# Retention scores and a Mish feed-forward on one core: block 2 of 11 takes the form that block 3 has

## The chip, the cores and the metric

The kernel runs on one core of one Trainium2 chip, as one launch. Its time is device microseconds of that core. Five engines take part, each with an instruction stream of its own that it works through in order: PE (TensorE, matmuls and weight loads), DVE (VectorE), ACT (ScalarE), POOL (GpSimd) and SP (SyncE, which here only issues DMAs). They wait for each other through semaphores: an instruction that waits holds up all that stands behind it on its engine.

## What is computed

`q`, `k` and `v` are (4, 8, 768, 64): 4 batches, 8 heads, 768 positions, 64 numbers each. A decaying state is updated at each position and read by `q`; the heads side by side give `x` of 3072 rows by 512. Then a feed-forward with Mish follows, with weights of 512x2048 and 2048x512.

```python
state = np.zeros((B, H, D, D), dtype=np.float32)
for t in range(S):
    state = gamma[None, :, None, None] * state + np.einsum('bhd,bhe->bhde', k[:, :, t], v[:, :, t])
    y[:, :, t] = scale * np.einsum('bhd,bhde->bhe', q[:, :, t], state)
x = attn_out.transpose(0, 2, 1, 3).reshape(B * S, H * D)
h = x @ w_in
sp = np.where(h > 20.0, h, np.log1p(np.exp(np.minimum(h, 20.0))))
return (h * np.tanh(sp)) @ w_out
```

## The kernel before

**Tiling.** The 768 positions of a batch are 6 chunks of 128, so there are 24 chunks, numbered 0 to 23 through all batches. They are worked in 11 blocks: block 0 has chunks 0 to 3, block n from 1 on has chunks 2n+2 and 2n+3. Block 2 thus has chunks 6 and 7, block 3 has 8 and 9, block 4 has 10 and 11, block 5 has 12 and 13. Chunk 11 is the last of batch 1 (`last_of_batch`), chunk 9 is not.

**The small matmuls.** For a block, 64x64 matmuls make the outer products of `k` and `v` (`outers`, L515, into the tile `u`, and of these DVE makes the states), the scores (`scores`, L507, into `at`) and then `y` in three parts: `past_of` from the states, `present_of(own)` and, after a wait for a DVE copy (`seen`, L660), the other half of `present_of` (all at L621). The scores are masked by DVE (`mask_two`, L604 or L609) before `present_of` reads them. The states after a block's second chunk come from `leave`, that is `state_of` (L570 to L581): an addition (L579) that reads `u`, and a product (L580). For the last chunk of a batch `state_of` returns before both.

**The feed-forward.** Both products are done with sums that save an eighth of the matmuls. The first (`full_in`, L973) takes 112 matmuls of 128x128 in groups, the second (`seven`, L1098, or `full_out`, L1215) 56 of 128x256. DVE makes the sums that the second needs: `sums_a` (L925, L926), `sums_b` (L930) and `sums_c` (L934).

**Where a block's small matmuls stand.** This is set by two numbers, `ONE, BACK = 3, 4`, and there are three forms:

- Blocks before `ONE` (1 and 2): the outer products and the scores of the next block stand inside this block's first product, by `get_ready` (L583), which ends with `settle` (the states, on DVE). `y` of the next block stands in `seven`, and is cut in two by half of a product of 256 columns.
- Block `ONE` (3): the same `get_ready` of block 4, and in `seven` the whole of `y` of block 4 with the outer products and scores of block 5 (`retain(4, 5)`, which calls `ready(5)`) in one piece.
- Blocks from `BACK` (4) on: no `get_ready`; in `full_out` the same piece, `retain(blk + 1, blk + 2)`.

**Banks of PSUM.** Up to block `BACK` the tiles `at` and `u` of a block share the pool `atps`. For blocks after `BACK`, `hold` (L530) closes that pool and opens two new ones in its place (`new_banks`), so their first tiles lie on the banks of the last `at` and `u` of `atps`: the writer waits until those have been read.

**Conversions and loads.** SP loads `q`, `k`, `v` of a chunk, POOL converts them (`casts_qk`: L440 for `q` and L454 for `k`; `casts_v`: L459), ACT takes some of the `k` (`cast_k`, L452), and a transposing DMA from SP (`turn_by_dma`, L464) turns `q` and `k` for the scores. The outer products read the converted `k` and `v` directly. POOL is held back in places by a copy of one column to `summed`: it waits for the DVE instruction that writes that column, and the conversions stand behind it. In `cast_load` (called at the head of block 2) chunk 10 is converted and the loads of 12 and 13 issued; `cast_behind(2, 3)` and the lines at L1152 and L1169 take chunks 11, 12 and 13.

**Matmuls cut in halves.** `IN_HALVES` and `HALVED` name products whose matmuls are issued as two of half the columns, each with a weight load.

Of the kernel before, what the change touches and what calls it, by code (L numbers as in the profile page):

```python
# [16 lines left out]
def kernel(  # L17
# [9 lines left out]
    nc = tc.nc  # L27
    B, H, S, D = q.shape
    d_model, d_ff = moe_w_in.shape
    P = 128  # L30
# [4 lines left out]
    TB = 512  # L35
# [84 lines left out]
    loaded, cast, qkts, ats, ams, states, mids, us, ys = {}, {}, {}, {}, {}, {}, {}, {}, {}  # L120
    xts, gts, wins, wouts, wtmps = {}, {}, {}, {}, {}
    gtiles, tmats, gsums = {}, [], []
    ONE, BACK = 3, 4
    EVEN, ODD = slice(0, NBP, 2), slice(1, NBP, 2)
    ROWS = [[slice(i, i + 1) for i in (0, 2, 1, 3)], [EVEN, ODD], [EVEN, ODD], [slice(0, NBP)]]
    whole, late_k = {}, []
    HALVED, DEFER = {6: (8, 8, 0, 0, 0)}, 6
    IN_HALVES = {0: range(NFB - 7, NFB), 1: range(NFB - 8, NFB)}
    FULL, SUMS_AT = (2, 3), {1: (4, 5, 5, 6)}
    in_makes = {}  # L130
    nload, ncast = [0], [0]
# [829 lines left out]
    def full_in(blk, last):  # L961
# [62 lines left out]
        for fn, p in ((first_of, 0), (first_of, 1), (fifth_of, 0), (fifth_of, 1)) if both else (  # L1024
                (first_of, 0), (fifth_of, 0), (first_of, 1), (fifth_of, 1)):
            fn(p)
        if late_k:
            g = first[blk] + 5
            store(1)
            cast_k(*late_k.pop(0))  # L1030
            turn_by_dma(g)
            casts_v(g - 1)
            casts_v(g)
            load_to(g + 3)
            store(1)
        settled = last or both
        if both:
            leave(blk)
# [32 lines left out]
        for p in two:  # L1071
            mm(pa[p], a(p, 1, 1), t[3])
            mish(p, 1, 0, pa[p])
        sums_a(blk, 1)

    def seven(blk, masks, hooks):
        n, hf = NFB // 2, d_model // 2
        px = pxps.tile([P, hf], FP32, name="o_ps", tag="px")
        pb = mmps.tile([P, hf], FP32, name="o_ps", tag="mm")
        osb = [  # L1080
            op.tile([P, d_model], FP32, name="osb", tag="osb", bufs=9) for _ in range(2)]

        def a(i, j):
            return lambda f: gts[blk, j * n + f][:, i * P:(i + 1) * P]

        def b(i, j):
            return lambda f: wouts[(i * n + f) // FPS][:, f % FPS, j * hf:(j + 1) * hf]

        def s(i):
            return lambda f: gsums[blk % 2][:, i - 1, f]  # L1090

        def t(i):
            return lambda f: tmats[(i - 1) // 2][:, (i - 1) % 2, f]

        def mm(o_ps, x, w, first=False, turn=0, part=slice(None), cols=slice(None)):
            for z in range(n)[part]:
                f = (z + turn) % n
                nc.tensor.matmul(  # L1098
                    o_ps[:, cols], x(f), w(f)[:, cols], start=first and z == 0, stop=z == n - 1,
                    skip_group_check=True)  # L1100

        def snap(o_ps, cols=slice(0, hf)):
            x = op.tile([P, hf], FP32, name="snap", tag="snap", bufs=3)[:, cols]
            nc.scalar.copy(x, o_ps[:, cols])
            return x

        def done(i, j, o_ps, plus=None, cols=slice(0, hf)):
            at = slice(j * hf + cols.start, j * hf + cols.stop)
            dst = osb[i][:, at]
            if plus is None:  # L1110
                nc.vector.tensor_copy(dst, o_ps[:, cols])
            else:
                nc.vector.tensor_tensor(dst, o_ps[:, cols], plus, op=ALU.add)

        def call(fns):
            for fn, *args in fns:
                fn(*args)

        mm(px, a(0, 0), b(0, 0), True)
        m1 = snap(px)  # L1120
        mm(pb, a(0, 1), b(1, 0), True)
        if blk < ONE:
            sums_b(blk)
            if blk == 1:
                cast_behind(blk, 2)
            sums_c(blk)
            if blk > 1:
                cast_behind(blk, 3)
            done(0, 0, pb, m1)
            call(masks)  # L1130
        else:
            done(0, 0, pb, m1)
            call(masks)
            sums_b(blk)
        pe = mmps.tile([P, hf], FP32, name="o_ps", tag="mm")
        mm(pe, s(1), t(1), True)
        m5 = snap(pe)
        mm(px, s(2), t(2))
        u2 = snap(px)
        for _ in late_k[:2 if blk == 1 else 1]:  # L1140
            cast_k(*late_k.pop(0))
        if blk < ONE:
            mm(pe, s(4), b(1, 1))
            call(hooks[0])
            call(hooks[1])
            done(0, 1, pe, u2)
            mm(px, s(3), t(3), part=slice(0, n // 2))
            call(hooks[2][:1])
            mm(px, s(3), t(3), part=slice(n // 2, n))
            pl = mmps.tile([P, hf], FP32, name="o_ps", tag="mm")  # L1150
            u3 = snap(px)
            if late_k:  # L1152
                cast_k(*late_k.pop(0))
                turn_by_dma(first[blk] + 6)
            done(1, 1, px, m5)
            if blk + 1 in FULL:
                x_sums(blk + 1, slice(0, 1))
            else:
                call(hooks[2][1:])
            mm(pl, a(1, 1), t(4), True)  # L1160
            done(1, 0, pl, u3)
            if blk + 1 in FULL:
                x_sums(blk + 1, slice(1, 3))
            if blk == 1:
                g = first[blk] + 4
                nc.gpsimd.tensor_copy(summed, xts[blk + 1][:, 2, TB - 1:])
                casts_v(g + 1)
                sum_input(1)
            elif late_k:  # L1169
                g = first[blk] + 7  # L1170
                nc.gpsimd.tensor_copy(summed, xts[blk + 1][:, 2, TB - 1:])
                casts_qk(g, False)
                casts_v(g - 3)
                late_k[0] = (g, True, loaded[g][1])
        else:
            call(hooks[0])
            sums_c(blk)
            cast_behind(blk, 3)
            call(hooks[1])
            mm(px, s(3), t(3))  # L1180
            done(1, 1, px, m5)
            call(hooks[2])
            mask_two(blk + 2, slice(0, 1))
            mm(pe, s(4), b(1, 1))
            x_sums(blk + 1, slice(0, 2))
            done(0, 1, pe, u2)
            mm(px, a(1, 1), t(4))
            done(1, 0, px)
            mask_two(blk + 2, slice(1, 2))
            x_sums(blk + 1, slice(2, 4))  # L1190
        for i in range(2):
            stores.append((1 + i, out_rows(blk, i), osb[i]))
# [355 lines left out]
        load_to(g + 4)  # L1548

    def cast_load(g):  # L1550
        casts_qk(g)
        ncast[0] = g + 1
        both = (g + 2, g + 3)
        for n in both:
            room(n)
            load_one(n, 0, nc.sync)
            load_one(n, 1, nc.sync)
        nload[0] = g + 4

    def turn_four(g):  # L1560
        for n in range(2):
            turn_by_dma(g + n)
        for n in (2, 3):
            load_one(g + n, 2, nc.sync)

    def cast_behind(blk, i):
        g = first[blk] + (6 if blk == 1 else 8)
        if ncast[0] < min(g, NCK):
            nc.gpsimd.tensor_copy(summed, gsums[blk % 2][:, i, NFB // 2 - 1, P - 1:])  # L1569
            if blk == 1:  # L1570
                for n in range(g - 2, g):
                    casts_qk(n, False)
                    late_k.append((n, True, loaded[n][1]))
                casts_v(g - 2)
                ncast[0] = g
            elif blk + 1 >= BACK:
                cast_to(g - 2)
                casts_qk(g - 2, blk > ONE)
                if blk == ONE:
                    cast_k(g - 2, True)  # L1580
                ncast[0] = g
            else:
                late = ncast[0] if blk < ONE else None
                for n in range(ncast[0], g):
                    on_act = late is not None
                    if n < g - 1 or not on_act:
                        casts_qk(n, not on_act)
                    if on_act:
                        late_k.append((n, True, loaded[n][1]))
                    if late is not None and n == late + 1:  # L1590
                        casts_v(late)
                for n in range(g - 2, g) if late is None else ():
                    casts_v(n)
                ncast[0] = g

    def plan_of(blk):
        a = first[blk] + 4
        plan = {u: [] for u in (0, 1, 5, 6)}
        plan[6 if blk == 1 else 5] = [(get_ready, blk + 1)]
        if blk == 1:  # L1600
            plan[0] += [(load_to, a + 2)]
            plan[1] += [(begin_load, a + 2)]
        elif blk < ONE:
            plan[1] += [(cast_load, a)]
        return plan

    first_block()
    for blk in range(1, len(BLOCKS)):
# [11 lines left out]
        for u in range(0 if blk in FULL else NFB // 2):  # L1620
# [7 lines left out]
            for _ in range(SUMS_AT[blk].count(u)):  # L1628
# [1 line left out]
        later = blk + 2 if blk == ONE else None  # L1630
        hooks = [([(leave, blk + 1)] if later is not None else []) + [(retain, blk + 1, later)],
                 [(next_one, first[blk] + 6)] if blk + 1 >= BACK else
                 [(turn_load, first[blk] + 4)] if blk == 1 else
                 [(turn_four, first[blk] + 4)],
                 [(finish, blk + 1)] if later is None else []]
        if later is None:
            hooks[2].append((leave, blk + 1))
# [32 lines left out]
```

## Time and profile before

| | us |
|---|---|
| median of 3 runs | 190.83 (190.58 to 190.96) |
| the profiled execution | 190.31 |
| its span, from the first to the last instruction | 188.5 |
| mean granted TensorE clock | 1.000 |
| DVE busy in the span | 148.6 |
| ACT busy | 113.0 |
| POOL busy | 66.3 |

The page of the profile gives for each engine its busy time, and a chain of waits: from the last instruction back to what released it, step by step. The chain's listing has one row for each piece, with its start, its length and how many instructions it holds. A timeline gives one engine's instructions with start, duration, line and shapes. For a DMA, a row of its tile gives the time from issue to landing. A matmul's row tells when its columns enter and when its last result is out, so rows of neighbours overlap: between two such pieces, compare starts with starts.

### The profile page before, as it was taken

Reading aid. Unit: us, or ns where it says so; the run is one execution under the profiler, and the core shown is the slowest. Engines: PE = TensorE matmul, PEld = TensorE weight load, DVE = VectorE, ACT = ScalarE, POOL = GpSimd, SP = SyncE. Lnnn points to the kernel's source line nnn. Section 1 sums busy time; section 2 is a strip of 40 time slices with the busy share of each in tenths; the row PEclk is TensorE's granted clock in tenths of the full one; section 3 lists DMA queues with packets and bytes.
Section 4 is the critical chain, followed back from the end, with each engine's and each line's share of the span. In section 5 each row is a group of like instructions: output and inputs, shape, how many; then the busy total and the mean of one; then the engine's idle time right before and its main releaser. Section 6 shows DMA issues by size and latency. Waiting matters only on the chain.

```text
span 188.5 us, 7969 instructions
## 1 busy us (share of the span) xinstructions
PE 182.3 (97%) x3438; PEld 162.2 (86%) x3438; DVE 148.6 (79%) x318; ACT 113.0 (60%) x217; POOL 66.3 (35%) x95
## 2 busy tenths in 40 slices
PE   7898999999999999999999999999999999999993
PEld 7556478888998998998998998998998998988983
DVE  0888599999987998997897697687698698666862
ACT  3575776254655583884684583683673773874651
POOL 5072000578507516532354614714624800000000
PEclk9999999999999999999999999999999999999999
DMA  5999999999999999999999996993999982301103
GB/s 165 309 311 389 384 385 368 299 324 221 170 246 205 197 239 145 173 257 219 235 136 242 174 199 146 158 280 76 223 222 230 198 291 76 116 3 46 68 3 111
DMA packets 83235, 38.84 MB, mean 206 GB/s; under 512 B 58240, under 2 KB 76288, under 8 KB 83200
## 3 DMA queue, kind: packets, MB, share of 16 engines
q1 hardware_dynamic: 82912, 38.22, 88.4%
q8 instruction: 27, 0.44, 1.0%
q10 hardware_dynamic: 288, 0.11, 0.3%
q14 instruction: 8, 0.07, 0.1%
HBM read 27.31 MB, written 6.29 MB: 178 GB/s over the span
## 4 chain that ended last, share of the span: by engine, by line
PE 92%; DMA 3%; SPq 1%; POOL 1%; issue 1%; ACT 0%; DVE 0%; POOLq 0%; DVEq 0%
PE h_ps L973 30%; PE o_ps L1215 23%; PE o_ps L1098 10%; PE h_ps L753 8%; PE o_ps L810 7%; DMA kf<-in_k_dram 3%; PE y_ps L621 3%; PE h_ps L700 2%; PE at L507 2%; PE u_ps L515 1%; PE y_ps L399 1%; POOL qk L320 1%; PE h_ps L736 1%; PE t_ps L267 1%; PE at L350 1%
## 5 line engine op out<-in xcount | busy, mean ns | idle before, releaser
L973 PE MATMUL h_ps<-xt,wsum 128*128 128x128 f16 x576 | 37.5, 219 | 0.0
L985 ACT ACTIVATE g<-h_ps 128x512 f16<-128x512 f32 x54 | 30.8, 599 | 7.1 <-PE h_ps L973 7.1
L973 PEld LDWEIGHTS <-wsum 128*128 128x128 f16 x576 | 33.6, 98 | 0.0
L973 PE MATMUL h_ps<-xt,win 128*128 128x128 f16 x432 | 31.2, 219 | 0.0
L973 PEld LDWEIGHTS <-win 128*128 128x128 f16 x432 | 26.3, 98 | 0.4
L1215 PEld LDWEIGHTS <-gsum 128*128 128x128 f16 x232 | 21.5, 98 | 2.6
L1215 PE MATMUL o_ps<-tmat,gsum 128*128 128x256 f16 (+1 forms) x176 | 21.5, 268 | 0.0
L1046 DVE TENSOR_TENSOR h_ps<-h_ps,hsum 128x512 f32<-128x512 f32 x18 | 12.5, 693 | 9.5 <-PE h_ps L973 9.4
L440 POOL TENSOR_TENSOR qk<-qf,qvs 128x512 f16<-128x512 f32 x18 | 19.0, 1062 | 0.9 <-DMA qf<-in_q_dram 0.8
L459 POOL TENSOR_TENSOR v<-vf,qvs 128x512 f16<-128x512 f32 x18 | 18.7, 1054 | 1.4 <-DMA vf<-in_v_dram 1.4
L1016 ACT COPY h_ps<-h_ps 128x512 f32<-128x512 f32 x18 | 10.5, 582 | 13.4 <-issue 8.7
L1215 PEld LDWEIGHTS <-g 128*128 128x128 f16 x184 | 16.5, 98 | 1.6
L679 ACT CAST xt<-y_ps 128x512 f16<-128x512 f32 x16 | 10.8, 738 | 9.5 <-PE y_ps L621 8.2
L753 PE MATMUL h_ps<-xt,win 128*128 128x256 f16 (+2 forms) x164 | 16.3, 260 | 0.0
L753 PEld LDWEIGHTS <-win 128*128 128x128 f16 x164 | 13.4, 98 | 2.7
L1569 POOL COPY summed<-gsum 128x1 f16<-128x1 f16 x7 | 1.6, 234 | 39.4 <-DVE gsum L934 32.0
L1225 ACT COPY snap<-o_ps 128x256 f32<-128x256 f32 (+1 forms) x22 | 8.2, 374 | 11.0 <-PE o_ps L1215 11.0
L1215 PE MATMUL o_ps<-wout,g 128*128 128x256 f16 (+1 forms) x120 | 14.5, 265 | 0.0
L762 ACT ACTIVATE g<-h_ps 128x512 f16<-128x512 f32 x18 | 10.7, 597 | 6.0 <-PE h_ps L753 6.0
L998 DVE TENSOR_TENSOR hsum<-h_ps,hsum 128x512 f32<-128x512 f32 x18 | 12.4, 686 | 0.9 <-PE h_ps L973 0.2
L810 PEld LDWEIGHTS <-g 128*128 128x128 f16 x120 | 11.4, 98 | 1.6
L454 POOL TENSOR_TENSOR qk<-kf,qvs 128x512 f16<-128x512 f32 x12 | 12.7, 1061 | 0.0
(130 smaller groups left out, 347.8 us busy)
## 6 DMA issues: line engine op xcount, KB each, us to landing
out_dram<-osb SPq DMA_DIRECT2D x22, 256.0 KB, 3.6
qf<-in_q_dram SPq DMA_DIRECT2D x18, 256.0 KB, 5.3
kf<-in_k_dram SPq DMA_DIRECT2D x14, 256.0 KB, 6.0
vf<-in_v_dram SPq DMA_DIRECT2D x14, 256.0 KB, 5.4
wt<-in_moe_w_out_dram SPq DMA_DIRECT2D x6, 512.0 KB, 8.6
vf<-in_v_dram SPq DMA_DIRECT2D x20, 128.0 KB, 4.3
wi<-in_moe_w_in_dram SPq DMA_DIRECT2D x4, 512.0 KB, 8.8
kf<-in_k_dram SPq DMA_DIRECT2D x16, 128.0 KB, 4.2
```

The lines of the kernel that those rows point to most:

```text
L440: nc.gpsimd.tensor_tensor(in_place(q16.rearrange("p (w x) d -> p w x d", x=2)), by_head(qf), scale_by_head(qs_two[:, heads]), op=ALU.mult)
L454: nc.gpsimd.tensor_tensor(dst, src, boosts.rearrange("p (w y) -> p w y", y=2).unsqueeze(3).broadcast_to((P, H // 2, 2, D)), op=ALU.mult)
L459: nc.gpsimd.tensor_tensor(cast[g][2], loaded.pop(g)[2], vs[g % 2].unsqueeze(2).broadcast_to((P, H, D)), op=ALU.mult)
L679: nc.scalar.copy(dst[:, :, x], src)
L753: nc.tensor.matmul(h_ps[:, j, cols], wins[s][f // 2][:, bp, f % 2 * P:(f % 2 + 1) * P], xts[blk][:, bp, cols], start=(bp == 0 and at == 0) ...
L810: nc.tensor.matmul(banks[ij][:, t], x(f)[:, t * P:(t + 1) * P], w(f), start=ij in open_banks, stop=f == fs[-1], skip_group_check=True)
L973: nc.tensor.matmul(o_ps[:, f], w(f // 2, k)[:, f % 2 * P:(f % 2 + 1) * P], x[:, k], start=begin and f == 0 and k == 0, stop=k == 1, skip_g ...
L985: nc.scalar.activation(gt[:, f:f + n, j * C:(j + 1) * C], src, AF.Mish, scale=inv_boost3)
L998: nc.vector.tensor_tensor(m, src, plus, op=ALU.add)
L1046: nc.vector.tensor_tensor(pf[p], pa[p], m5[p], op=ALU.add)
L1098: nc.tensor.matmul(o_ps[:, cols], x(f), w(f)[:, cols], start=first and z == 0, stop=z == n - 1, skip_group_check=True)
L1215: nc.tensor.matmul(o_ps[:, c:c + wide], x(f), w(f)[:, c:c + wide], start=first and f == 0 and c == cols.start, stop=f == n - 1, skip_group ...
```

## The change

`ONE` and `BACK` go down by one. Block 2 gets the form of block 3: in its `seven`, `retain(3, 4)` has `y` of block 3, the outer products and the scores of block 4 in one piece. Block 3 gets the form of the blocks behind it, through `full_out`. The new pools of PSUM are opened for block 4 in place of block 5. Chunks 10 and 11 are both converted at the head of block 2, `q` and `k` at once and `v` after the second `sums_a`; the loads of 12 and 13 stand behind both transposes. The halved matmuls are spread anew: 4 fewer of 512 columns are cut in block 0 and 32 fewer of 256 columns in block 1; 24 more of 256 columns are cut in block 2 and 12 more in block 3, so that PE has as many instructions as before.

```diff
-    ONE, BACK = 3, 4
+    ONE, BACK = 2, 3
...
-    HALVED, DEFER = {6: (8, 8, 0, 0, 0)}, 6
-    IN_HALVES = {0: range(NFB - 7, NFB), 1: range(NFB - 8, NFB)}
+    HALVED, DEFER = {3: (8, 4, 0, 0, 0), 6: (8, 8, 0, 0, 0)}, 6
+    IN_HALVES = {0: range(NFB - 6, NFB), 1: ()}
...
     def full_in(blk, last):
...
-        if late_k:
-            g = first[blk] + 5
-            store(1)
-            cast_k(*late_k.pop(0))
-            turn_by_dma(g)
-            casts_v(g - 1)
-            casts_v(g)
-            load_to(g + 3)
-            store(1)
...
         sums_a(blk, 1)
+        if blk == ONE:
+            nc.gpsimd.tensor_copy(summed, gsums[blk % 2][:, 1, NFB // 2 - 1, P - 1:])
+            for g in (4, 5):
+                casts_v(first[blk] + g)
...
     def seven(blk, masks, hooks):
...
-            mm(px, s(3), t(3))
+            mm(px, s(3), t(3), wide=hf // 2)
...
-            mm(pe, s(4), b(1, 1))
+            mm(pe, s(4), b(1, 1), wide=hf // 2)
...
-            mm(px, a(1, 1), t(4))
+            mm(px, a(1, 1), t(4), wide=hf // 2)
...
     def cast_load(g):
-        casts_qk(g)
-        ncast[0] = g + 1
-        both = (g + 2, g + 3)
-        for n in both:
-            room(n)
-            load_one(n, 0, nc.sync)
-            load_one(n, 1, nc.sync)
-        nload[0] = g + 4
-
-    def turn_four(g):
         for n in range(2):
+            casts_qk(g + n)
             turn_by_dma(g + n)
+        ncast[0] = g + 2
+        for n in (2, 3):
+            room(g + n)
+            load_one(g + n, 0, nc.sync)
+            load_one(g + n, 1, nc.sync)
         for n in (2, 3):
             load_one(g + n, 2, nc.sync)
+        nload[0] = g + 4
```

The rest of the diff takes away the branches for a block 2 that comes before `ONE` (in `seven` and `cast_behind`).

Three places of the order in which the instructions stand. On PE, where the outer products begin behind the first part of `y`, before in block 3 (`y` of block 4, `u` of block 5; a semaphore's name begins with the engine, or the DMA queue, that raises it):

```order
L621 LDWEIGHTS v_1732
L621 MATMUL y_ps<-am,v_1732 64x64
L515 LDWEIGHTS qk_1734
L515 MATMUL u_ps<-v_1735,qk_1734 64x64 [waits Pool_49]
```

And now the same place in block 2 (`y` of block 3, `u` of block 4):

```order
L621 LDWEIGHTS v_1297
L621 MATMUL y_ps<-am,v_1297 64x64
L515 LDWEIGHTS qk_1437 [waits DVE_49,Pool_49]
L515 MATMUL u_ps<-v_1438,qk_1437 64x64 [waits Pool_49]
```

The first weight load of the outer products now waits for DVE as well; the count that it waits for in the built program is the one that the addition of `leave` raises (L579 of block 3's second chunk, the row below). It reads block 3's `u`, on whose banks block 4's `u` now lies. Before, the block in this place was block 4, whose second chunk ends a batch, so there is no such addition.

On DVE, from the last `sums_a` of the block to `sums_c`, before in block 3:

```order
L926 TENSOR_TENSOR gsum<-gsum,g 128x512 [waits DVE_49]
L1113 TENSOR_TENSOR osb<-o_ps,snap 128x256 [waits PE_49,Activation_49]
L609 TENSOR_TENSOR am<-at,tri_half 128x1024
L930 TENSOR_TENSOR gsum<-g 128x1024 [waits Pool_49]
L660 COPY seen<-y_ps 128x1 [waits PE_49]
L934 TENSOR_TENSOR gsum<-g,gsum 128x1024 [waits DVE_49]
```

And now in block 2:

```order
L926 TENSOR_TENSOR gsum<-gsum,g 128x512 [waits DVE_49]
L1109 TENSOR_TENSOR osb<-o_ps,snap 128x256 [waits PE_49,Activation_49]
L609 TENSOR_TENSOR am<-at,tri_half 128x1024
L930 TENSOR_TENSOR gsum<-g 128x1024
L579 TENSOR_TENSOR suh<-u_ps,mid 128x256
L580 TENSOR_TENSOR sth<-suh,gch 128x256 [waits DVE_49]
L660 COPY seen<-y_ps 128x1 [waits PE_49]
L934 TENSOR_TENSOR gsum<-g,gsum 128x1024
```

`leave` of block 3 (L579, L580) now stands between `sums_b` and the copy that the second part of `y` waits for.

On POOL, from the conversion of chunk 10's `k` to that of chunk 11's `v`, now (L1067 is the new copy to `summed`; `qk_1437` and `v_1438` are chunk 10, `qk_1443` and `v_1444` chunk 11):

```order
L454 TENSOR_TENSOR qk_1437<-kf,qvs 128x4x2x64 [waits DMAHW0_49]
L440 TENSOR_TENSOR qk_1443<-qf,qvs 128x2x4x64 [waits DMAHW4_49,PE_49]
L454 TENSOR_TENSOR qk_1443<-kf,qvs 128x4x2x64 [waits DMAHW5_49]
L1067 COPY summed<-gsum 128x1 [waits DVE_49,Pool_49]
L459 TENSOR_TENSOR v_1438<-vf,qvs 128x512 [waits DMAHW1_49]
L459 TENSOR_TENSOR v_1444<-vf,qvs 128x512 [waits DMAHW6_49]
```

Before, chunk 11's `q` was converted after `sums_c` of block 2 and its `k` by ACT; the `v` of 10 and 11 came in block 3.

More of the change, by code (lines that the diff above doesn't have):

```diff
@@ L1093, in t, with mm @@
             return lambda f: tmats[(i - 1) // 2][:, (i - 1) % 2, f]
[L1095 to L1100, printed above, removed]
+        def mm(o_ps, x, w, first=False, part=slice(None), wide=hf):
+            for f in range(n)[part]:
+                for c in range(0, hf, wide):
+                    nc.tensor.matmul(
+                        o_ps[:, c:c + wide], x(f), w(f)[:, c:c + wide],
+                        start=first and f == 0 and c == 0, stop=f == n - 1,
+                        skip_group_check=True)
         def snap(o_ps, cols=slice(0, hf)):
@@ L1123, in seven @@
             sums_b(blk)
-            if blk == 1:
-                cast_behind(blk, 2)
+            cast_behind(blk, 2)
             sums_c(blk)
-            if blk > 1:
-                cast_behind(blk, 3)
             done(0, 0, pb, m1)
@@ L1139, in seven @@
         u2 = snap(px)
-        for _ in late_k[:2 if blk == 1 else 1]:
+        for _ in late_k[:]:
             cast_k(*late_k.pop(0))
@@ L1151, in seven @@
             u3 = snap(px)
-            if late_k:
-                cast_k(*late_k.pop(0))
-                turn_by_dma(first[blk] + 6)
             done(1, 1, px, m5)
@@ L1163, in seven @@
                 x_sums(blk + 1, slice(1, 3))
[L1164 to L1174, printed above, removed]
+            nc.gpsimd.tensor_copy(summed, xts[blk + 1][:, 2, TB - 1:])
+            casts_v(first[blk] + 5)
+            sum_input(1)
         else:
@@ L1581, in cast_behind @@
                 ncast[0] = g
[L1582 to L1594, printed above, removed]
     def plan_of(blk):
@@ L1602, in plan_of @@
             plan[1] += [(begin_load, a + 2)]
-        elif blk < ONE:
+        elif blk == ONE:
             plan[1] += [(cast_load, a)]
@@ L1632 @@
                  [(next_one, first[blk] + 6)] if blk + 1 >= BACK else
-                 [(turn_load, first[blk] + 4)] if blk == 1 else
-                 [(turn_four, first[blk] + 4)],
+                 [(turn_load, first[blk] + 4)],
                  [(finish, blk + 1)] if later is None else []]
```

## Prediction

> **What bounds the kernel now.** First the page: its span, the engines' shares, and the chain of waits by engine.
>
> ```profile
> span 188.5 us, 7969 instructions
> PE 182.3 (97%) x3438; PEld 162.2 (86%) x3438; DVE 148.6 (79%) x318; ACT 113.0 (60%) x217; POOL 66.3 (35%) x95
> PE 92%; DMA 3%; SPq 1%; POOL 1%; issue 1%; ACT 0%; DVE 0%; POOLq 0%; DVEq 0%
> ```
>
> PE is busy 97% of the span and is 92% of the chain that ended last. Then the same chain in order of time (start, length, piece), from block 2 to the head of block 6:
>
> ```profile
> 62.05 5.40 PE h_ps L973 x96
> ...
> 76.20 5.41 PE h_ps L973 x96
> ...
> 90.75 6.30 PE h_ps L973 x112
> 97.05 3.51 PE o_ps L1215 x32
> ...
> 101.00 0.32 PE u_ps L515 x32
> 101.32 0.53 PE at L507 x32
> ...
> 104.73 6.33 PE h_ps L973 x112
> ...
> 118.54 6.30 PE h_ps L973 x112
> ```
>
> The rows follow each other without a wait for another engine: here every nanosecond taken from PE's stream is a nanosecond of the result, and every wait put into it too. A block lasts from one first product's row to the next: block 2 is 76.20 - 62.05 = 14.15, block 3 is 90.75 - 76.20 = 14.55, block 4 is 13.98 and block 5 is 118.54 - 104.73 = 13.81. So two things decide: what PE's stream gets shorter by, and whether what it needs is there when it gets there.
>
> **The change part by part.** *PE's stream.* Block 2 takes block 3's form: 14.55. Block 3 takes the form of blocks 4 and 5; block 4's 13.98 has 0.21 more than the 0.32 that the outer products beside them take in the scores' row (0.53), with no releaser, so I take block 5's 13.81. Blocks 2 and 3 had 14.15 + 14.55 = 28.70 and get 14.55 + 13.81 = 28.36, less by 0.34. What goes is two separate groups of small matmuls (the cut of `y` in block 2, block 4's own group in block 3), not a matmul.
>
> *Halves.* 32 pairs fewer in block 1, 24 + 12 more in blocks 2 and 3. A pair costs 2 x 6.30/112 = 0.1125 against 3.51/32 = 0.1097 whole, so 0.003 each: 4 pairs more net, 0.01. The four of 512 columns in block 0 go the other way, by as little. PE's stream: -0.33.
>
> *The new wait.* The outer products of block 4 now wait for L579 on DVE. When does PE get there, and when DVE? PE by the starts of its timeline, block 3 first, then block 2:
>
> ```profile
> 83.07 1.91 PE L1098 MATMUL o_ps<-wout,g 128*128 128x256 f16 x16
> ...
> 87.06 0.49 PE L515 MATMUL u_ps<-v,qk 64*64 64x64 f16 x32
> ```
>
> ```profile
> 68.96 1.91 PE L1098 MATMUL o_ps<-wout,g 128*128 128x256 f16 x16
> ```
>
> In block 3 the outer products start 87.06 - 83.07 = 3.99 after the second product does. Block 2's second product starts at 68.96 (its first product stays as it was), so PE would be there at 72.95. DVE in block 3, which has the same order up to L930, and then block 5, where L579 stands behind L930:
>
> ```profile
> 85.08 0.42 DVE L1113 TENSOR_TENSOR osb<-o_ps,snap 128x256 f32<-128x256 f32 x1
> 85.43 1.21 DVE L609 TENSOR_TENSOR am<-at,tri_half 128x1024 f16<-128x1024 f32 x1
> 86.56 0.68 DVE L930 TENSOR_TENSOR gsum<-g 128x1024 f16<-128x1024 f16 x1
> ```
>
> ```profile
> 112.24 0.69 DVE L930 TENSOR_TENSOR gsum<-g 128x1024 f16<-128x1024 f16 x1
> 112.84 0.42 DVE L579 TENSOR_TENSOR suh<-u_ps,mid 128x256 f32<-128x256 f32 x1
> ```
>
> L930 starts 86.56 - 83.07 = 3.49 into the second product, in block 2 at 72.45; L579 starts 0.60 later (73.05) and ends 0.42 after that, at 73.47. DVE works without a pause from L1113 on, and L1113 waits for a product of PE, so none of this can come sooner. To that 0.1 for the wake-up: PE's first matmul behind a DVE copy in the chain comes at 16.35, the copy ended at 16.30, and here a weight load stands between. So at best 73.57, a stall of 0.62.
>
> ```profile
> 16.13 0.17 DVE seen L1393
> 16.30 0.04 issue
> 16.35 0.42 PE y_ps L399 x16
> ```
>
> *POOL beside it.* The two `v` conversions now start behind the last L926 of block 2. Its row, and how POOL went on behind such a wait in the same block before (it waited for L934, which ended at 72.05):
>
> ```profile
> 70.43 0.42 DVE L926 TENSOR_TENSOR gsum<-gsum,g 128x512 f16<-128x512 f16 x1
> ...
> 71.37 0.68 DVE L934 TENSOR_TENSOR gsum<-g,gsum 128x1024 f16<-128x1024 f16 x1
> ```
>
> ```profile
> 72.19 0.19 POOL L1569 COPY summed<-gsum 128x1 f16<-128x1 f16 x1 [5.54 <-DVE gsum L934]
> 72.33 2.04 POOL L440 TENSOR_TENSOR qk<-qf,qvs 128x512 f16<-128x512 f32 x2
> ```
>
> The second conversion ended at 74.37, 2.32 after DVE. So `v` of chunk 10 ends near 72.17, chunk 11 at 70.85 + 2.32 = 73.17: late for its outer products by about 0.1, if nothing else were. But L930 (72.45) falls into the second conversion. What that does to a DVE instruction with both inputs in SBUF stands at 48 us, where the same shape takes 0.68 alone:
>
> ```profile
> 48.12 0.93 DVE L909 TENSOR_TENSOR tmat<-wout 128x1024 f16<-128x1024 f16 x1
> 49.15 1.37 DVE L910 TENSOR_TENSOR tmat<-wout,tmat 128x1024 f16<-128x1024 f16 x1
> 50.45 0.68 DVE L911 TENSOR_TENSOR tmat<-wout,wout 128x1024 f16<-128x1024 f16 x1
> ```
>
> ```profile
> 47.46 1.04 POOL L459 TENSOR_TENSOR v<-vf,qvs 128x512 f16<-128x512 f32 x1
> 48.93 1.04 POOL L459 TENSOR_TENSOR v<-vf,qvs 128x512 f16<-128x512 f32 x1 [0.43 <-DMA vf<-in_v_dram]
> ```
>
> L909 ends at 49.05, POOL's conversion at 48.50; L910 ends at 50.52, POOL's at 49.97: both 0.55 after POOL. So L930 ends at 73.17 + 0.55 = 73.72, L579 runs from 73.63 to 74.05, and PE goes on at 74.15: a stall of 1.20 from the 72.95. Bounds: 0.62 if POOL took nothing from DVE, 1.33 if L930 did all its 0.68 after POOL. I take 1.20, since the two rows are the same shape and agree to 0.01. [...]
>
> Behind PE's wait stand its outer products, scores, the second part of `y` and three products; all later blocks follow with it, since PE never waits later in the chain and so cannot catch up. The second part of `y` waits for L660, which comes after L580 (if that takes 0.4 as L579 does, to 74.5); PE gets there 2 x 0.32 after 74.15, at 74.8: no second stall. That also covers `v` of chunk 11.
>
> *Chunk 11's transpose.* Its `k` was issued at 63.34, as it will be; it lands 4.5 later, at 67.9. POOL is free at 66.65 (row below), so it converts `k` by 69.0. SP has the transpose next.
>
> ```profile
> 65.56 1.09 POOL L454 TENSOR_TENSOR qk<-kf,qvs 128x512 f16<-128x512 f32 x1
> ```
>
> ```profile
> DMA to landing us min/median/max: 4.5/4.5/4.5
> ```
>
> ```profile
> DMA to landing us min/median/max: 3.7/4.3/5.1
> ```
>
> The first of these is that load's, the second that of the six transposes between 59 and 80 us: 69.1 + 4.3 = 73.4, at most 74.2. The scores get to it at 74.5: covered by the stall, by nothing else. The loads of 12 to 14 go out behind it, from about 70.4 in place of 64.5; block 3 needs their outcome only near 87, so I cost that at nothing; without that cover it would be what comes late of it.
>
> Sum: -0.33 + 1.20 = +0.87. The profiled execution has 190.31 (1.8 outside its span, unchanged), so 191.18; it lies 0.52 under the median of the runs, which gives 190.83 + 0.87 = **191.7 us**.
>
> **The rivals.** *The merge pays* (no wait on L579 in time): the wait's count stands for an earlier reader of the bank, the mask L609, which ends at 72.53. Then PE never stops there, and what is left is 190.83 - 0.33 = 190.5. For it: the mask is the reader that all other blocks have. Against it: the count, and that `u` is read last by L579. It decides if L579 ends before 72.95, and then chunk 11's `v` and transpose still lie within 0.1 of need. *POOL does not hold DVE*: stall 0.62, so 191.1. For it: L579 and L609 read PSUM and their rows do not stretch beside POOL; against it: L930 reads SBUF alone. *A late transpose*: of the two issued near 92 and 95 us the slower took 6.2 (the answer below; it is the longest of the three answers). With that, chunk 11's comes at 75.3, and PE waits some 0.85 more: 192.5.
>
> ```profile
> DMA to landing us min/median/max: 4.6/5.4/6.2
> ```
>
> *PE's own gaps*: the 0.21 in block 4 has no releaser, and PE's instructions in blocks 1 to 3 now lie elsewhere in its stream. Unknown; such a gap could go (-0.21) or a further one come (+0.21). I take 0.
>
> **How the numbers follow.** The forecast has 0.55, with 191.4 to 192.0 as its own range; the merge that pays 0.18, POOL apart 0.12, the late transpose 0.10, and 0.05 for something else. The range leaves out a little of both ends: 190.5 to 192.5. What can be told from no change here is about 0.2%, 0.38 us: the forecast (0.46%) and the late transpose are slower, 191.1 is the same, and 190.5 lies on the border, so half of it counts as faster and half as same. With the last 0.05 shared, that is slower 0.67, same 0.20, faster 0.13.
>
> **What would show it.** In the chain of the changed kernel one group of small matmuls less in block 2 and in block 3, and block 3 near 13.8. In block 2 a gap on PE between the first part of `y` and L515, ended by DVE's L579, of about 1.2, and block 2 at 15.8; L930 there at 1.2 or more in place of 0.68, ending 0.55 after POOL's second `v`. If L930 stays at 0.68, POOL was priced wrongly; if there is no gap before L515, the wait was, and the time is near 190.5. A gap before L507 instead means the transpose.

## The result and the profile after

The changed kernel takes 192.43 us (median of 4 runs, 192.19 to 192.56), the one before beside it 190.73 (190.58 to 190.96): a ratio of 1.0087, 95% interval 1.0069 to 1.0104. It is slower by 1.70 us; the forecast was 0.87 slower, at 191.7, with 191.4 to 192.0 as its own range and 190.5 to 192.5 as the whole one. The profiled execution took 192.19 us, 1.9 of it outside its span.

First the page of the changed kernel: span, the engines' busy time, the queue that brings PE's instructions, and the chain by engine.

```profile
span 190.3 us, 7965 instructions
...
PE 182.2 (96%) x3438; PEld 162.0 (85%) x3438; DVE 147.6 (78%) x318; ACT 111.8 (59%) x214; POOL 69.6 (37%) x99
...
q8 instruction: 27, 0.44, 1.0%
...
PE 91%; DMA 3%; DVE 2%; issue 1%; ACT 1%; SPq 0%; DVEq 0%
```

PE has as many matmuls as before and is busy for as long (182.2 against 182.3), in a span that is 1.8 longer. So nothing became slower on PE; it stood still. Where, the waits of PE show (who waited, for whom: us in total, times, longest), and then the chain in order of time (start, length, piece) from block 2 on:

```profile
PE u_ps L515 <- DVE suh L579: 1.1, 1, 1.1
PE o_ps L1093 <- issue: 1.0, 1, 1.0
```

```profile
61.99 5.40 PE h_ps L973 x96
...
69.06 1.76 PE o_ps L1093 x16
...
70.91 0.42 DVE osb L1109
71.33 1.13 DVE am L609
72.46 1.18 DVE gsum L930
73.64 0.34 DVE suh L579
73.98 0.14 issue
74.12 0.38 PE u_ps L515 x20
...
74.96 2.12 PE o_ps L1093 x36
77.07 0.96 issue
78.03 0.84 PE o_ps L1093 x12
78.88 6.30 PE h_ps L973 x112
...
92.74 6.30 PE h_ps L973 x112
...
106.52 6.30 PE h_ps L973 x112
```

Read by first products, block 2 is now 78.88 - 61.99 = 16.89 (14.15 before), block 3 is 13.86 (14.55) and block 4 is 13.78 (13.98). That is +2.74 - 0.69 - 0.20 = +1.85, the whole difference. In block 2 PE stops twice. The first gap is the predicted one: the matmuls of `y` (L621) start every 17 ns or so until 72.86, the outer products would follow at 72.88 and come at 74.12, 1.24 late, behind L579. The second lies in the last of the halved products, between its fourth matmul and its fifth: the fourth starts at 76.85, the next was due 0.06 later and starts at 78.03, 1.12 late. No engine releases it ("issue"). 14.55 + 1.24 + 1.12 = 16.91, against the 16.89.

**What stands at the second gap.** Queue q8 brings PE's instructions: 27 packets, of 16,384 bytes each. Counted in order of start (matmuls, weight loads and the 9 semaphore and drain instructions, 6,885 in all), the first instruction behind the gap is PE's 2,498th. In the same profile PE has one other such stop of that size that nothing releases, before its 450th instruction at 15.44 us, and 2,498 - 450 = 2,048 = 8 x 256. From the records of q8, the start of the fetch that came last before each of the two:

```
instruction   fetch starts   PE's last before   PE goes on   gap    from the fetch's start
450           12.74          14.53              15.44        0.91   2.69
2,498         75.53          76.86              78.03        1.17   2.50
```

So the reading to test (theory F) was: PE's instructions come in blocks of 256, the next block is fetched only about when PE enters the last one that it has, or later (here PE entered at instruction 2,242, at 72.70), and a block can be used 2.4 to 2.8 us after its fetch starts. In the kernel before the same block's fetch began at 72.08, and PE needed it 5.75 later. In the changed one it began at 75.53, when PE was 1.3 us from the end. That q8 serves PE fits the counts too: 27 packets with 6,885 instructions, which reach past the 6,850th (450 + 25 x 256), and 26 in the kernels below with 6,837 or 6,789, which don't.

### The profile page after: what moved, and what is told of

It reads as the page before. It is cut to its first block, busy times and chain, and to the rows that moved or that the text cites. A ratio compares the mean times of both kernels' runs of the same rounds, so it can differ in the third digit from the quotient of the medians.

```text
span 190.3 us, 7965 instructions
## 1 busy us (share of the span) xinstructions
PE 182.2 (96%) x3438; PEld 162.0 (85%) x3438; DVE 147.6 (78%) x318; ACT 111.8 (59%) x214; POOL 69.6 (37%) x99
## 4 chain that ended last, share of the span: by engine, by line
PE 91%; DMA 3%; DVE 2%; issue 1%; ACT 1%; SPq 0%; DVEq 0%
PE h_ps L973 30%; PE o_ps L1197 26%; PE h_ps L753 8%; PE o_ps L810 7%; PE o_ps L1093 6%; DMA kf<-in_k_dram 3%; PE y_ps L621 3%; PE h_ps L700 2%; PE u_ps L515 2%; PE at L507 1%; PE t_ps L267 1%; PE at L350 1%; PE y_ps L399 1%; PE h_ps L736 1%; ACT qkt L271 1%
## 5 line engine op out<-in xcount | busy, mean ns | idle before, releaser
L973 PE MATMUL h_ps<-xt,wsum 128*128 128x128 f16 x576 | 37.7, 219 | 0.0
L985 ACT ACTIVATE g<-h_ps 128x512 f16<-128x512 f32 x54 | 31.0, 597 | 7.3 <-PE h_ps L973 7.3
L973 PEld LDWEIGHTS <-wsum 128*128 128x128 f16 x576 | 33.6, 98 | 0.0
L973 PE MATMUL h_ps<-xt,win 128*128 128x128 f16 x432 | 31.5, 219 | 0.0
L1197 PEld LDWEIGHTS <-gsum 128*128 128x128 f16 x268 | 24.6, 98 | 2.9
L973 PEld LDWEIGHTS <-win 128*128 128x128 f16 x432 | 26.5, 98 | 0.3
L1197 PE MATMUL o_ps<-tmat,gsum 128*128 128x256 f16 (+1 forms) x204 | 24.7, 267 | 0.0
L1197 PEld LDWEIGHTS <-g 128*128 128x128 f16 x216 | 19.0, 98 | 1.8
L679 ACT CAST xt<-y_ps 128x512 f16<-128x512 f32 x17 | 11.4, 742 | 10.1 <-PE y_ps L621 10.1
L1207 ACT COPY snap<-o_ps 128x256 f32<-128x256 f32 (+1 forms) x25 | 9.4, 374 | 12.6 <-PE o_ps L1197 12.6
L1197 PE MATMUL o_ps<-wout,g 128*128 128x256 f16 (+1 forms) x144 | 16.6, 260 | 0.0
L753 PE MATMUL h_ps<-xt,win 128*128 128x256 f16 (+1 forms) x128 | 16.2, 286 | 0.0
L454 POOL TENSOR_TENSOR qk<-kf,qvs 128x512 f16<-128x512 f32 x15 | 15.9, 1057 | 0.1
L753 PEld LDWEIGHTS <-win 128*128 128x128 f16 x128 | 12.4, 98 | 3.4
L1220 DVE TENSOR_TENSOR osb<-o_ps,snap 128x256 f32<-128x256 f32 (+1 forms) x25 | 10.4, 415 | 5.0 <-ACT snap L1207 2.8
```

Of the source, the lines that this page charges most:

```text
L454: nc.gpsimd.tensor_tensor(dst, src, boosts.rearrange("p (w y) -> p w y", y=2).unsqueeze(3).broadcast_to((P, H // 2, 2, D)), op=ALU.mult)
L679: nc.scalar.copy(dst[:, :, x], src)
L753: nc.tensor.matmul(h_ps[:, j, cols], wins[s][f // 2][:, bp, f % 2 * P:(f % 2 + 1) * P], xts[blk][:, bp, cols], start=(bp == 0 and at == 0) ...
L973: nc.tensor.matmul(o_ps[:, f], w(f // 2, k)[:, f % 2 * P:(f % 2 + 1) * P], x[:, k], start=begin and f == 0 and k == 0, stop=k == 1, skip_g ...
L985: nc.scalar.activation(gt[:, f:f + n, j * C:(j + 1) * C], src, AF.Mish, scale=inv_boost3)
L1197: nc.tensor.matmul(o_ps[:, c:c + wide], x(f), w(f)[:, c:c + wide], start=first and f == 0 and c == cols.start, stop=f == n - 1, skip_group ...
```

## The experiments

All edits are to the changed kernel. In kernels with added lines, names move: L579 is L588 there, L930 is L942, L660 is L672, L973 is L985 and L1093 is L1105 (and in kernel 7, L959 is L971 and L1197 is L1210). The kernel before ran beside each group: 190.36 (20 runs) for the first four, 190.46 (17) for the next three, 190.23 (7) for the last two.

**1. L579 ahead of L930** (which `sums_b` issues); `leave_first` issues L579 alone, `leave_rest` L580.

```diff
         call(masks)
+        leave_first(blk + 1)
         sums_b(blk)
...
-hooks = [([(leave, blk + 1)] if later is not None else []) + [(retain, blk + 1, later)],
+hooks = [[(retain, blk + 1, later)] + ([(leave_rest, blk + 1)] if later is not None else []),
```

> Edit to the changed kernel: L579 (the first half of what `leave` does) is issued on DVE ahead of L930, L580 behind the group of small matmuls. Every theory of the first wait: the gap before block 2's outer products falls from 1.24 us to 0.1 to 0.3, since L579 no longer stands behind L930. They differ on the total. Theory F (the second gap, inside the third product, is PE waiting for its next block of 256 instructions, which a DMA queue of its own brings at a moment that does not depend on how early PE comes): that gap grows by what the first lost, from 1.12 to about 2.2, PE resumes at about the same 78.0 us, and the time stays at 192.4 (192.0 to 192.7). Theory A (two costs that add up: the second gap has a fixed length): the second gap stays 1.1 and the time falls to 191.3.

192.27 us (10 runs, 191.22 to 194.07), ratio 1.0099 (1.0066 to 1.0132). The chain:

```profile
72.45 0.33 DVE suh L588
72.79 0.84 DVE gsum L942
73.63 0.08 DVE seen L672
...
76.19 1.79 issue
77.97 0.84 PE o_ps L1105 x12
78.82 6.30 PE h_ps L985 x112
```

The wait for L579 is gone: the outer products start at 72.97 in place of 74.12. A wait of 0.23 for L660, which stands behind L930, is left. PE comes to the halved product 0.89 earlier, stops at the same instruction, 2,498, and goes on at 77.97 in place of 78.03. A second gap of fixed length would have given 191.3. So the two gaps don't add up: the second ends when the block arrives, and the first had hidden 0.9 of its lateness.

**2. Whole products again.**

```diff
-mm(px, s(3), t(3), wide=hf // 2)
+mm(px, s(3), t(3))
```

and so for the other two products.

> Edit to the changed kernel: the three products of block 2 that were issued as pairs of 128 columns are issued whole (256 columns) again, 24 matmuls and 24 weight loads fewer. Theory F (instruction blocks): PE uses up its block later, by about 33 x 0.055 = 1.8 us, the fetch is there by then, the second gap is gone; the first stays at 1.24: 192.43 - 1.12 = 191.3 (191.1 to 191.5). Rival H (the halves themselves are slow behind the small matmuls, by bank or by write): also gone, same time. Rival W (PE waits for something of DVE, ACT or a transfer that the profile does not show): the gap stays near 78 us, at a product issued whole, and the time at 192.4.

192.49 (5 runs), ratio 1.0093 (1.0054 to 1.0131). PE's timeline shows that the second gap of block 2 went as expected (no stop near 78 us, so rival W is out), the first one stayed, and that the time came back in block 4:

```profile
73.96 0.38 PE L515 MATMUL u_ps<-v,qk 64*64 64x64 f16 x20 [1.12 <-DVE suh L579]
...
76.48 1.04 PE L1093 MATMUL o_ps<-tmat,g 128*128 128x256 f16 x8
77.36 0.61 PE L973 MATMUL h_ps<-xt,win 128*128 128x128 f16 x8
```

```profile
103.06 0.38 PE L507 MATMUL at<-qkt 64*64 64x64 f16 x24 [0.86 <-DMA qkt<-qk]
```

The last product runs on into block 3. But in block 4 the scores now wait 1.04 us for a transpose, that of chunk 15. In the changed kernel it landed at 101.43 and PE came to the scores at 103.14; here it was issued at 97.35, landed at 103.02, and PE had come for it at 102.0. A further stop, of 0.54 and without a releaser, stands before PE's 4,802nd instruction, 9 x 256 behind the 2,498th. With 48 instructions fewer ahead of it, the block that ends there holds others: PE used it up in 2.19 us (128.77 to 130.96), and in 3.66 in the changed kernel. So the cause of the second gap is as expected, and the time is not: it lies 1.0 above the expected 191.1 to 191.5.

**3. Both edits.**

> Both edits: L579 ahead of L930, and the three products whole. Theory F: first gap 0.1 to 0.3; without the 1.24 of the first gap PE reaches the end of its instruction block 1.1 us earlier than in the run with whole products alone, about 77.6 against a fetch that is in at about 78.0, so a rest of 0 to 0.5 may be left of the second gap: 190.2 to 190.8. Theory A (the costs add up): 192.43 - 1.1 - 1.12 = 190.2.

191.88 (10 runs, 190.43 to 192.42), ratio 1.0061 (1.0034 to 1.0087). The chain has both later stops:

```profile
76.84 0.67 PE h_ps L985 x12
77.51 0.23 issue
77.74 5.80 PE h_ps L985 x100
...
97.31 5.74 DMA qkt<-qk
103.05 0.04 issue
103.09 0.38 PE at L507 x24
```

The rest of the gap for instructions lies behind the twelfth matmul of block 3, another product with other operands. With 24 matmuls and 24 weight loads fewer ahead of it, that is the 2,498th instruction again. The transpose costs 1.16, which the expected 190.2 to 190.8 had not counted.

**4. The loads of chunks 12 and 13 later**, in `load_two`, which is called behind the two `v` conversions.

```diff
             for g in (4, 5):
                 casts_v(first[blk] + g)
+            load_two(first[blk] + 4)
...
         ncast[0] = g + 2
+
+    def load_two(g):
         for n in (2, 3):
             room(g + n)
+            if n == 2:
+                nc.gpsimd.memset(loaded[g + n][0][:, 0, 0, :1], 0.0)
             load_one(g + n, 0, nc.sync)
```

> Edit to the changed kernel: the six loads of chunks 12 and 13 go out behind the second `v` conversion (a one-element write by POOL into the first load's tile holds them back), from about 73.3 us in place of 70.5; PE's instructions and the halves stay. Theory F with the DMA queues as the reason (the fetch stood behind the loads' packets from 72.7 to 75.5): the fetch starts within 0.7 us of PE's entering the last block, PE's second gap is gone, first gap unchanged: 191.3 (191.1 to 191.6). Rival H (the halves are slow): the gap stays 1.1 and the time 192.4. Chunk 12's later load may delay its transpose, but that one had 2 us to spare in block 3.

193.14 (4 runs), ratio 1.0129 (1.0087 to 1.0172). What the queues did between PE's entering the block (72.7) and 75.5, in the changed kernel and then here (q1 carries the loads; packets, MB, and their time as a share of 16 engines):

```profile
q1 hardware_dynamic: 2196, 0.73, 106.9%
```

```profile
q1 hardware_dynamic: 416, 0.21, 27.6%
q8 instruction: 1, 0.02, 2.3%
```

With the loads held back (no packet of theirs before 73.4) the fetch starts 0.80 us after PE entered the block (73.47), in place of 2.83, and the gap is gone with all halves in place: the last product runs through from 76.96. That the halves are slow is thereby out. The time, expected at 191.1 to 191.6, is worse for three other waits: the first grew to 1.54, since POOL's conversions ended at 73.36 here, and the later loads made the transposes late for block 3's and block 4's scores (0.67 and 1.02).

**5 and 6. The late transpose ahead of the loads**, on SP, with both edits (5) and with whole products alone (6).

```diff
-if blk != DEFER:
+if blk not in (ONE + 1, DEFER):
     load(g + 3 + ahead)
...
     turn_by_dma(g + 1)
+    if blk == ONE + 1:
+        load(g + 3)
```

> Edit to the kernel with both edits (L579 ahead of L930, products whole): on SP the second transpose of block 4's second group (issued behind five load issues, at 97.3 us, landed 5.7 us later, where PE waited 1.16 us for it at its scores) goes out ahead of those five. Theory S (the time won in block 2 was lost again at that transpose, which stood behind the loads on SP and on the DMA queues): it is issued at about 94.1, lands at 98 to 100, the wait at 101.9 is gone, and the time is 191.88 - 1.16 = 190.7 (190.4 to 191.0). Rival D (the transpose lands late whatever is ahead of it, since the queues are full): it lands at 101.5 or later and more than half of the wait stays: 191.4 to 191.9.

> The changed kernel with the products of block 2 whole and that transpose ahead of the five load issues, but with L579 behind L930 as in the change. What is left is the first wait alone, 1.24 to 1.30 us, no gap for an instruction block in block 2 and none at the transpose: theory S gives 192.49 - 1.04 = 191.4 (191.1 to 191.6). If the first wait costs what its gap shows, the kernel beside it, with L579 ahead of L930, is faster by about 0.7 (1.3 less 0.23 that it keeps and 0.39 that its instruction block costs it).

Kernel 5: 191.42 (10 runs, 190.28 to 192.49), ratio 1.0036 (1.0011 to 1.0061). Kernel 6: 191.32 (8 runs, 191.05 to 192.13), ratio 1.0050 (1.0032 to 1.0068). SP in kernel 5:

```profile
94.04 1.28 SPq L464 DMA_TRANSPOSE qkt<-qk  x1
95.38 0.57 SPq L174 DMA_DIRECT2D qf<-in_q_dram  x1
```

The transpose goes out at 94.04 and lands 4.9 later; the wait in block 4 is gone from both profiles, and theory S holds for it. The profiled execution of kernel 5 took 190.43, within the expected 190.4 to 191.0, with small stops left: 0.23 for L660, 0.17 for instructions. But its runs spread over 2.2 us, their median lies 0.4 above that range, and the 0.7 by which it should lead kernel 6 isn't in the medians. Kernel 6 met its 191.1 to 191.6 in the median, but not by the parts expected: in its profile (191.69) the load of chunk 10's `q` came later, the first wait was 1.68, and a stop of 0.27 stands before the 4,802nd instruction.

**7. No halves in block 0**, on top of kernel 5.

```diff
-IN_HALVES = {0: range(NFB - 6, NFB), 1: ()}
+IN_HALVES = {0: (), 1: ()}
```

> The kernel with L579 ahead of L930, whole products and the early transpose, and in block 0 no matmuls in halves (24 matmuls and 24 weight loads fewer ahead of block 2, so that the end of the instruction block lies 24 matmuls later, 1.3 us at that place). Theory F: the rest of the gap for the instruction block (0.39 us at the twelfth matmul of block 3) is gone, since the fetch comes by the loads on the DMA queues and not by PE; the time is 0.4 below that of the kernel beside it, 190.3 (190.0 to 190.6). If that gap was tied to its place in block 3, it stays at the twelfth matmul.

192.41 (4 runs), ratio 1.0089 (1.0066 to 1.0112), against 190.0 to 190.6 expected. The gap at instruction 2,498 shrank from 0.17 to 0.07, but two others came:

```profile
89.02 0.38 PE L507 MATMUL at<-qkt 64*64 64x64 f16 x24 [1.55 <-DMA qkt<-qk]
...
133.61 0.61 PE L1210 MATMUL o_ps<-tmat,g 128*128 128x256 f16 x4 [0.71 <-DVE xt L971]
```

The first is a transpose for block 3's scores that was issued at 84.30, behind five loads and another transpose, and landed at 88.98. The second the profile puts down to DVE; but that DVE row (xt, L971) had ended 0.30 us before PE went on, and the stop stands at PE's 4,802nd instruction, 2.37 us after a fetch began. So I read it as a block that came late. The other traces bear this out: in kernels 2, 3, 5, 6, 8 and 9, which have 48 instructions fewer than the changed one, PE stops before its 4,802nd too, for 0.03 to 0.54, 2.4 to 3.0 us after a fetch, and in the changed kernel, 1 and 4 it doesn't. No run takes this stop away by itself.

**8 and 9. POOL's conversions off L930**: with whole products and the early transpose (8), and with L579 ahead as well (9).

```diff
-nc.gpsimd.tensor_copy(summed, gsums[blk % 2][:, 1, NFB // 2 - 1, P - 1:])
 for g in (4, 5):
     casts_v(first[blk] + g)
```

> The kernel with whole products and the early transpose, L579 behind L930, and the gate ahead of the two `v` conversions of POOL left out, so that they follow the `k` conversion at once (about 69.1 to 71.2 us) and no longer lie beside L930. Theory P (L930 is held by POOL's conversions until 0.55 us after they end): L930 takes 0.68 again; the first wait falls from 1.24 to 0.6 if L925 and L926, which the conversions now lie beside, are done by 71 us all the same; if they are held (one until 0.55 after POOL's end, 71.7), the third product and the mask come up to 1 us later and the wait moves there: time 190.8 (190.4 to 191.6). Rival L (L930 is long for a reason of its own in this place): L930 stays at 1.2 or more and the wait before the outer products at 1.2 or more.

> As the kernel beside it, with L579 ahead of L930 as well. Theory P with no harm at L925 and L926: no wait of more than 0.1 before the outer products and before the second part of y (the 0.23 that stood there went with L930's end at 73.6), 190.2 (189.9 to 190.6), at or below the kernel before. If L925 and L926 are held: a wait of 0.3 to 1 at the third product, 190.5 to 191.2.

Kernel 8: 192.40 (4 runs), ratio 1.0099 (1.0070 to 1.0129). Kernel 9: 192.18 (4 runs), ratio 1.0092 (1.0056 to 1.0128). DVE and then PE in kernel 8:

```profile
69.70 1.15 DVE L926 TENSOR_TENSOR gsum<-gsum,g 128x512 f16<-128x512 f16 x1
70.77 1.26 DVE L925 TENSOR_TENSOR gsum<-g 128x512 f16<-128x512 f16 x1
...
73.87 0.68 DVE L930 TENSOR_TENSOR gsum<-g 128x1024 f16<-128x1024 f16 x1
```

```profile
72.08 1.48 PE L1092 MATMUL o_ps<-tmat,gsum 128*128 128x256 f16 x12 [0.89 <-DVE gsum L925]
...
75.03 0.38 PE L515 MATMUL u_ps<-v,qk 64*64 64x64 f16 x20 [0.71 <-DVE suh L579]
```

L930 is back at 0.68, so theory P holds and L is out; the wait for L579 falls from 1.24 to 0.88. The hold moved to L925 and L926, which take 1.15 and more in place of 0.42, and PE loses 1.05 a product earlier. In kernel 9 the wait for L579 is 0.28, that for L925 (L937 there) is 0.88 and those for instructions are 0.5 in block 3 and 0.27 before the 4,802nd.

All nine kernels are slower than the kernel before: every interval lies above 1. The expected times did worse than the expected causes: only kernels 1 and 6 met theirs; the other seven lie 0.4 to 1.8 us above the top of their ranges, and in the profiles of all of these but kernel 5 another stop came or grew.

## Why the prediction was right, and where it fell short

The direction and the first wait were right. That 192.43 lies in the whole range is luck: it is outside the forecast's own 191.4 to 192.0, and the range went up to 192.5 only for the rival of a late transpose, which did not come. The time was missed by one term, PE's own gaps.

- **The new wait: right in cause and size.** Forecast 1.20, measured 1.24. PE came to it at 72.88 (72.95 forecast), L930 ended at 73.64 (73.72), the outer products went on at 74.12 (74.15). That L579 causes it is shown by experiment 1.
- **POOL beside it: right.** From the timelines of the changed kernel, DVE first:

```profile
72.38 1.26 DVE L930 TENSOR_TENSOR gsum<-g 128x1024 f16<-128x1024 f16 x1
73.56 0.41 DVE L579 TENSOR_TENSOR suh<-u_ps,mid 128x256 f32<-128x256 f32 x1
```

```profile
71.05 2.04 POOL L459 TENSOR_TENSOR v<-vf,qvs 128x512 f16<-128x512 f32 x2
```

  POOL ends at 73.09, L930 at 73.64: 0.55 later, as the two rows before had it. In experiments 1, 2, 4 and 6, where POOL ended between 72.93 and 73.63, L930 ended 0.54 or 0.55 after it, and experiment 8 took the overlap away and got 0.68. The 1.33, with all of L930's 0.68 behind POOL, was not met: the 0.68 reach 0.13 back before the end of POOL's row. The rows of 128x512 (0.42 alone) that met a conversion in experiments 4, 6, 8 and 9 ended 0.27 or 0.28 after POOL, so they reach about as far back, 0.14 to 0.15. Whether DVE works beside POOL for that long, or POOL's hold ends before its row does, isn't shown.
- **PE's stream: right.** Block 3 is 13.86 (13.81 forecast), and block 2 without its gaps is 16.89 - 1.24 - 1.12 = 14.53 (14.55).
- **Chunk 11's transpose: covered**, landed at 72.33, before the outer products went on. So the rival of a late transpose was wrong for this place. It had the right kind of event: experiments 2 to 4 and 7 met it one and two blocks later, once PE was earlier (in experiment 4, the loads later). "The merge pays" fell with the wait that came, "POOL does not hold DVE" with L930's 1.26.
- **PE's own gaps: the term that was mis-sized.** The prediction named it, bounded it by the 0.21 without releaser in block 4 and took 0. Block 4's went (-0.20), and one of 1.12 came in block 2: +0.92 in place of 0. The bound came from the wrong row: the gap of 0.91 at 15.44 us stands in the profile of before too, with a fetch of q8 2.6 us ahead of it, and is a gap of this kind. Counting on from there in steps of 256 leads to the 2,242nd and the 2,498th instruction. It would have shown that the block between them now held the small matmuls from the outer products on (160 instructions in 0.8 us) and the halved products, while six loads were on the queues. In the kernel before PE took 6.25 us for the 256 instructions from 2,242 on (71.58 to 77.83); in the changed one 5.33, and without its two gaps 2.97. The sum with it, -0.33 - 0.20 + 1.24 + 1.12 = +1.83, is the +1.85 of the trace to 0.02.
- **"Since PE never waits later in the chain": too strong.** PE never waits in that profile, but there is little to spare: chunk 15's transpose landed 1.7 us before its use in the changed kernel, and came late in experiments 2 to 4. The stops hide one another, which is why undoing one of them returns little.
- **The chances.** By its own parts (0.12, and half of 0.18) "same" comes to 0.21 before its share of the last 0.05; the forecast wrote 0.20.

What stays open: why the runs of one kernel spread as they do (kernel 1 over 2.9 us, kernel 5 over 2.2). Each profile shows one execution, and the queues' timing differs in each; which stops the slower runs met wasn't seen.

## What to carry to other kernels

Before a change that packs many small instructions into a stretch, or cuts matmuls in halves, count the engine's instructions: find a gap in the trace that nothing releases, step on from it in blocks of 256 (the stops here lie at 450, 2,498 and 4,802), and see whether the stretch uses up a block faster than a fetch behind the loads of that moment can land (here PE was through in 4.16 us, from 72.70 to 76.86, and the fetch began 2.83 after the first of these, with PE going on 2.50 after that). When an engine that is busy for 97% of the span stops, take the next limit into the sum as well: a wait that goes may only uncover the one behind it, here a block of instructions (in experiment 1 PE came to it 0.89 earlier and went on 0.06 earlier) and then a transpose (1.16 in experiment 3). Moving POOL's conversions moved their hold on DVE with them here: in experiment 8 L930 went from 1.26 to 0.68, and an L926 and an L925 from 0.42 to 1.15 and 1.26. Beside DVE instructions that read PSUM it did no harm here: L609 took 1.22 beside POOL in the changed kernel and 1.21 without it in experiment 8.

## What the runs showed of the hardware

**Instruction blocks.** PE's instructions came in packets of 16,384 bytes. Where PE stopped for one, it stopped at instruction 450 + 256n, and went on 2.4 to 2.8 us after the fetch began (3.0 once, at the 4,802nd in experiment 2). In the eleven profiles a fetch began between 0.9 us before and 3.9 us after PE entered the last block that it had, so no run here shows PE with more than the next block ahead. For the 2,498th:

```
kernel              fetch starts   PE goes on   gap    from the fetch's start
before              72.08          77.83        0.05   5.75
changed             75.53          78.03        1.17   2.50
1 L579 ahead        75.42          77.97        2.00   2.55
2 whole             75.29          77.97        0.00   2.68
3 both              74.96          77.73        0.44   2.77
4 late loads        73.47          77.12        0.00   3.65
5 transpose first   74.66          77.41        0.17   2.75
6 whole, transpose  74.41          78.66        0.00   4.25
7 no halves, 0      76.13          78.54        0.07   2.41
8 v early           76.10          79.09        0.05   2.99
9 all               76.16          78.78        0.55   2.62
```

(Here a gap is counted from the start of the instruction before it, matmul or weight load; 0.05 is the usual distance there.) With the load queue at 27.6% between 72.7 and 75.5 us (experiment 4, idle until 73.4) the fetch began 0.80 us after PE had entered its last block, with it at 106.9% (changed kernel) 2.83 after.
